# A delta-rule attention and rational feed-forward kernel: VectorE does a share of Pool's unit steps, in a fixed order, and ScalarE makes first halves

## The chip, the cores and the metric

The kernel runs on one core of a Trainium2 chip. The metric is the device time of one execution in microseconds; several executions of the same program are timed, and the median is given.

## The reference

Two computations follow one another. The first is attention by the delta rule over 4 batches, 8 heads, 768 tokens and 48 channels per head; a state matrix is carried from token to token:

```python
k_n = k / (np.linalg.norm(k, axis=-1, keepdims=True) + 1e-06)
for t in range(S):
    kt, vt, bt = (k_n[:, :, t], v[:, :, t], beta[:, :, t, None])
    y[:, :, t] = np.einsum('bhd,bhde->bhe', q[:, :, t], state)
    v_old = np.einsum('bhde,bhd->bhe', state, kt)
    state = state + bt[:, :, :, None] * np.einsum('bhd,bhe->bhde', kt, vt - v_old)
```

Its output, as 3072 tokens of 384 channels, is the input of a feed-forward layer with 2048 hidden channels, whose activation is a quotient of polynomials:

```python
h = x @ w_in
P = a[0] + a[1] * h + a[2] * h**2 + a[3] * h**3
Q = 1.0 + np.abs(b[0]) * np.abs(h) + np.abs(b[1]) * h**2
out = (P / (Q + 1e-06)) @ w_out
```

## The kernel before, in words

The 768 tokens are cut into 12 chunks of 64. A chunk of all four batches makes 256 token columns (TG). The hidden channels are cut into 8 slices of 256, so the feed-forward part has 96 **units**, each one chunk and one slice. Matrix products run on TensorE in float16; for accuracy each operand is held as two float16 halves, a first half (the value rounded) and a second half (what the rounding left), and a product takes three passes.

One unit n goes through four functions:

- `hidden(n)`: TensorE makes h in a PSUM tile `ph` (two such tiles). Line L806.
- `numerator(n)`: ACT takes z = |B1 h| (L824); DVE makes w = (z + B0) h (L826); ACT makes u = A3 h + a2 (L828) and then |w| (L829); DVE makes u = h u (L830) and u = (u + A1) h (L831). These three DVE steps read `ph`; L831 is the last to do so, and sets it free.
- `quotient(n)`: ACT makes r = 1 / (w + Q0) as an exponential of a negative logarithm (L842, L843). DVE makes the first half g of the quotient (L848), then g times the denominator (L849), then what is missing of the numerator (L853); all three have their two tile operands in SBUF. Pool turns that into the second half (L854).
- `accumulate(n)`: TensorE multiplies with w_out into `po` (L869); after a chunk's last slice ACT copies the sum out (L883).

For a share of the units, `by_pool` (slices 0, 4, 5 and 6 of chunks 2 to 10, 36 units), Pool takes a part of DVE's steps: it adds A0 to u (L835), so that DVE's L848 becomes the plain product L846, and it does the subtraction (L851) instead of L853.

Around it the attention part of later chunks runs interleaved, one eighth of a chunk per unit (`attention`): `keys_normalized` and `queries_transposed` put keys and queries, split into halves by `transposed`, into one SBUF tile `kn`, which a DMA on SyncE's queue (SP) writes to DRAM as `xdk` or `xdq` (L461); another DMA brings them back transposed. `key_products` multiplies the keys with themselves (tile `g`, L519) and splits the product into `gl`. In `transposed` and `key_products` the first half is made by Pool (L226, the parameter `hi` of `split16`), and the second half, a subtraction, by Pool too (L232). Other splits let ACT make the first half (L228, L230). Other names: `rr` is the residual, `z` a step of the triangular solve, `mm` the masked query products, `xT` the feed-forward input, `wai`, `wao` and `wsi` belong to the weights, which are prepared in the prologue, the first 150 us.

The engines each run their instructions in one fixed order. That order is not written out: a scheduler works it out when the program is built, from the order in the code, priorities (`tc.high_priority`) and its own estimate of when each instruction becomes ready.

Of the kernel before, what the change touches and what calls it, by code (L numbers as in the profile page):

```python
# [36 lines left out]
def kernel(  # L37
# [138 lines left out]
    def zeroed(n, shape, dtype, nm, part=lambda t: t, eng=nc.gpsimd):  # L176
        made = []
        for i in range(n):
# [41 lines left out]

    S16 = cpool.tile([P, HP, D], F32, name="S16")

    def split16(dst, src, scale=None, eng=None, hi=None):

        if hi is not None:
            hi.tensor_scalar(dst[0], src, 1.0 if scale is None else scale, 0.0, op0=ALU.mult, op1=ALU.add)  # L226
        elif scale is None:
            nc.scalar.copy(dst[0], src)  # L228
        else:
            nc.scalar.activation(dst[0], src, AF.Copy, scale=scale)  # L230
        if scale is None:
            (eng or nc.vector).tensor_sub(dst[1], src, dst[0])  # L232
# [280 lines left out]
    def key_products(c):  # L513
        d = info[c]
        gd = d["gd"] = dpool.tile([P, BS], F32, tag="gd", name=f"gd_{c}")
        pg = bank(ps_f, f"pg_{c}", C)
# [2 lines left out]
        nc.scalar.mul(by_pair(g), pg[2], -1.0)  # L519
# [296 lines left out]
    def numerator(n):  # L816

        c, f2 = divmod(n, NU)
        d = unit[n]
# [4 lines left out]
        nc.scalar.activation(z, ph, AF.Abs, scale=B1)  # L824
# [1 line left out]
        nc.vector.scalar_tensor_tensor(out=w, in0=z, scalar=B0, in1=ph, op0=ALU.add, op1=ALU.mult)  # L826
# [1 line left out]
        nc.scalar.activation(u, ph, AF.Identity, scale=A3, bias=a2)  # L828
        nc.scalar.activation(w, w, AF.Abs)  # L829
        nc.vector.tensor_mul(u, ph, u)  # L830
        nc.vector.scalar_tensor_tensor(out=u, in0=u, scalar=A1, in1=ph, op0=ALU.add, op1=ALU.mult)  # L831

        by_pool = 2 <= c < NCH - 1 and f2 in (0, 4, 5, 6)
        if by_pool:
            nc.gpsimd.tensor_scalar(u, u, A0, 1.0, op0=ALU.add, op1=ALU.mult)  # L835
        d.update(u=u, w=w, r=r, A0=A0, Q0=Q0, by_pool=by_pool)

    def quotient(n):

        d = unit[n]  # L840
        u, w, r, A0, Q0, by_pool = (d.pop(x) for x in ("u", "w", "r", "A0", "Q0", "by_pool"))
        nc.scalar.activation(r, w, AF.Ln, bias=Q0)  # L842
        nc.scalar.activation(r, r, AF.Exp, scale=-1.0)  # L843
        g = sb.tile([P, 2, 2, TG], F16, tag="mg", name=f"mg{n}", bufs=MB)
        if by_pool:
            nc.vector.tensor_mul(g[:, 0], u, r)  # L846
        else:
            nc.vector.scalar_tensor_tensor(out=g[:, 0], in0=u, scalar=A0, in1=r, op0=ALU.add, op1=ALU.mult)  # L848
        nc.vector.scalar_tensor_tensor(out=w, in0=w, scalar=Q0, in1=g[:, 0], op0=ALU.add, op1=ALU.mult)  # L849
        if by_pool:  # L850
            nc.gpsimd.tensor_sub(u, u, w)  # L851
        else:
            nc.vector.scalar_tensor_tensor(out=u, in0=u, scalar=A0, in1=w, op0=ALU.add, op1=ALU.subtract)  # L853
        nc.gpsimd.tensor_mul(g[:, 1], u, r)  # L854
# [192 lines left out]
```

## Time and profile before

| what | us |
|---|---|
| median of 3 runs | 851.33 |
| lowest and highest | 850.73 to 855.22 |
| the profiled execution | 851.73 |
| its span, first to last instruction | 849.4 |
| chunks 2 to 8 of the units, from 297.5 | 423.1 |
| chunks 9 and 10, from 720.6 | 83.5 |
| chunk 11, from 804.1 | 45.3 |

The stages start with the first L824 of their chunk. In rows by line, a group shows its line, engine, operation, out<-in by tile names, shape, count, then its busy time and the mean of one in ns, then the idle time of the engine before them with what ended it. In rows in order of time the first number is the start and the second the duration in us; a bracket holds the idle time before and its releaser. PE is TensorE's matmuls, PEld its weight loads, DVE VectorE, ACT ScalarE, POOL GpSimd, SP the queue that issues DMAs.

### The profile page before, as it was taken

Reading aid. Unit: us, or ns where it says so; the run is one execution under the profiler, and the core shown is the slowest. Engines: PE = TensorE matmul, PEld = TensorE weight load, DVE = VectorE, ACT = ScalarE, POOL = GpSimd, SP = SyncE. Lnnn points to the kernel's source line nnn. Section 1 sums busy time; section 2 is a strip of 40 time slices with the busy share of each in tenths; the row PEclk is TensorE's granted clock in tenths of the full one; section 3 lists DMA queues with packets and bytes.
Section 4 is the critical chain, followed back from the end, with each engine's and each line's share of the span. In section 5 each row is a group of like instructions: output and inputs, shape, how many; then the busy total and the mean of one; then the engine's idle time right before and its main releaser. Section 6 shows DMA issues by size and latency. Waiting matters only on the chain.

```text
span 849.4 us, 23212 instructions
## 1 busy us (share of the span) xinstructions
PE 625.6 (74%) x9264; PEld 491.3 (58%) x9264; DVE 761.0 (90%) x1369; ACT 589.5 (69%) x1242; POOL 466.9 (55%) x430
## 2 busy tenths in 40 slices
PE   0230425777788678888868869879879889999885
PEld 0220425656466467666756747657657767787563
DVE  5999898799799889889978898897999999999886
ACT  3766667748575675886774866767677867887774
POOL 7665665464436556565564655664756546454522
PEclk9855556988999899999999989989989999999999
DMA  8987989959899968959879498379587583300000
GB/s 230 259 198 148 221 157 172 149 117 148 155 172 147 175 123 160 151 102 193 144 140 176 85 183 149 66 158 165 89 159 129 97 139 58 72 2 20 1 20 19
DMA packets 466507, 111.46 MB, mean 131 GB/s; under 512 B 431328, under 2 KB 463072, under 8 KB 466400
## 3 DMA queue, kind: packets, MB, share of 16 engines
q1 hardware_dynamic: 464224, 108.83, 69.7%
q8 instruction: 72, 1.18, 0.6%
q10 hardware_dynamic: 2176, 1.17, 0.5%
q14 instruction: 35, 0.29, 0.1%
HBM read 40.47 MB, written 26.23 MB: 79 GB/s over the span
## 4 chain that ended last, share of the span: by engine, by line
DVE 41%; ACT 14%; DMA 12%; PE 11%; issue 8%; SPq 8%; POOL 3%; POOLq 0%; ACTq 0%; DVEq 0%
DVE mw L849 4%; PE ph L806 4%; PE po L869 4%; DVE w_out L327 3%; DVE mw L826 3%; DVE mg L848 3%; DVE mu L830 3%; DVE mu L831 3%; DVE mu L853 2%; ACT mu L828 2%; DVE mg L846 2%; SPq L609 2%; DVE z L234 2%; ACT mr L824 2%; ACT kp L764 2%
## 5 line engine op out<-in xcount | busy, mean ns | idle before, releaser
L806 PE MATMUL ph<-xT,w_in 128*128 128x256 f16 x1728 | 224.2, 283 | 37.1 <-DVE mu L831 33.8
L869 PE MATMUL po<-w_out,mg 128*128 128x384 f16 x1152 | 223.4, 339 | 33.5 <-POOL mg L854 27.3
L806 PEld LDWEIGHTS <-w_in 128*128 128x128 f16 x1728 | 172.0, 102 | 76.4 <-DVE mu L831 24.9
L854 POOL TENSOR_TENSOR mg<-mu,mr 128x512 f16<-128x512 f32 x96 | 135.3, 1410 | 106.5 <-DVE mu L853 50.9
L869 PEld LDWEIGHTS <-mg 128*128 128x128 f16 x1152 | 110.6, 101 | 105.5 <-POOL mg L854 34.1
L828 ACT ACTIVATE mu<-ph,coef,msc 128x512 f32<-128x512 f32 x96 | 74.7, 778 | 54.4 <-DVE mw L826 54.2
L849 DVE SCALAR_TENSOR_TENSOR mw<-mw,msc,mg 128x512 f32<-128x512 f32 x96 | 92.6, 965 | 0.5
L851 POOL TENSOR_TENSOR mu<-mu,mw 128x512 f32<-128x512 f32 x36 | 51.0, 1418 | 72.5 <-DVE mw L849 38.3
L824 ACT ACTIVATE mr<-ph,msc 128x512 f32<-128x512 f32 x96 | 64.9, 682 | 36.9 <-POOL mg L854 11.5
L403 PEld LDWEIGHTS <-kbd 128*128 128x128 f16 x1680 | 60.8, 104 | 35.2 <-issue 33.4
L826 DVE SCALAR_TENSOR_TENSOR mw<-mr,msc,ph 128x512 f32<-128x512 f32 x96 | 70.4, 737 | 10.7 <-ACT mr L824 10.6
L831 DVE SCALAR_TENSOR_TENSOR mu<-mu,msc,ph 128x512 f32<-128x512 f32 x96 | 70.8, 739 | 1.1
L830 DVE TENSOR_TENSOR mu<-ph,mu 128x512 f32<-128x512 f32 x96 | 65.2, 680 | 5.6 <-ACT mu L828 4.6
L842 ACT ACTIVATE mr<-mw,msc 128x512 f32<-128x512 f32 x96 | 69.4, 724 | 0.9
L403 PE MATMUL pu<-z,ebd 128*128 128x48 f16 x1728 | 52.7, 186 | 19.4 <-DVE z L234 15.4
L848 DVE SCALAR_TENSOR_TENSOR mg<-mu,msc,mr 128x512 f16<-128x512 f32 x60 | 58.9, 982 | 6.2 <-ACT mr L843 5.7
L403 PEld LDWEIGHTS <-ebd 128*128 128x128 f16 x1728 | 51.7, 98 | 22.0 <-issue 20.8
L843 ACT ACTIVATE mr<-mr 128x512 f32<-128x512 f32 x96 | 60.2, 630 | 0.7
L829 ACT ACTIVATE mw<-mw 128x512 f32<-128x512 f32 x96 | 60.0, 625 | 0.0
L853 DVE SCALAR_TENSOR_TENSOR mu<-mu,msc,mw 128x512 f32<-128x512 f32 x60 | 52.1, 869 | 0.2
L835 POOL TENSOR_SCALAR mu<-mu,msc 128x512 f32<-128x512 f32 x36 | 28.1, 782 | 40.5 <-DVE mu L831 28.3
L232 POOL TENSOR_TENSOR mm<-m,mm 128x1024 f16<-128x1024 f32 x12 | 31.1, 2589 | 32.7 <-ACT mm L228 30.5
(198 smaller groups left out, 1306.3 us busy)
## 6 DMA issues: line engine op xcount, KB each, us to landing
wsi<-in_moe_w_in_dram SPq DMA_DIRECT2D x24, 256.0 KB, 5.2
xdk<-kn SPq DMA_DIRECT2D x24, 256.0 KB, 3.7
kbd<-tk SPq DMA_DIRECT2D x24, 256.0 KB, 5.1
gd<-g SPq DMA_DIRECT2D x24, 256.0 KB, 3.5
wso<-in_moe_w_out_dram SPq DMA_DIRECT2D x32, 192.0 KB, 4.0
xdq<-kn SPq DMA_DIRECT2D x24, 256.0 KB, 3.6
mbd<-mm SPq DMA_DIRECT2D x24, 256.0 KB, 5.4
wc<-img SPq DMA_DIRECT2D x24, 256.0 KB, 4.8
```

Source lines behind the costliest of these rows:

```text
L403: nc.tensor.matmul(dst[p][:, h], head(bd, lp, p * H + h), head(rt, rp, p * H + h), start=start and n == 0 and h == 0, stop=stop and n == l ...
L806: nc.tensor.matmul(ph[:, i], w_in[:, f2, wp, cc, i * P : (i + 1) * P], x[:, xp, cc], start=k == 0, stop=k == 3 * NCC - 1,)
L824: nc.scalar.activation(z, ph, AF.Abs, scale=B1)
L826: nc.vector.scalar_tensor_tensor(out=w, in0=z, scalar=B0, in1=ph, op0=ALU.add, op1=ALU.mult)
L828: nc.scalar.activation(u, ph, AF.Identity, scale=A3, bias=a2)
L830: nc.vector.tensor_mul(u, ph, u)
L831: nc.vector.scalar_tensor_tensor(out=u, in0=u, scalar=A1, in1=ph, op0=ALU.add, op1=ALU.mult)
L842: nc.scalar.activation(r, w, AF.Ln, bias=Q0)
L848: nc.vector.scalar_tensor_tensor(out=g[:, 0], in0=u, scalar=A0, in1=r, op0=ALU.add, op1=ALU.mult)
L849: nc.vector.scalar_tensor_tensor(out=w, in0=w, scalar=Q0, in1=g[:, 0], op0=ALU.add, op1=ALU.mult)
L854: nc.gpsimd.tensor_mul(g[:, 1], u, r)
L869: nc.tensor.matmul(po[p], g[:, gp, i, p * P : (p + 1) * P], w_out[:, f2, wp, i], start=f2 == lo and i == 0 and k == 0, stop=f2 == hi - 1 a ...
```

## The change

It has three parts. Pool's L835 and L851 and the special product L846 go, so that VectorE does L848, L849 and L853 for all 96 units. VectorE's six steps of the units carry one order token, which makes them run in the order in which the code names them: the three of numerator(n), then the three of quotient(n-1), then those of numerator(n+1). And the first halves of keys, queries and key products are made by ACT instead of Pool (36 instructions); Pool keeps the subtractions.

```diff
-    def split16(dst, src, scale=None, eng=None, hi=None):
-        if hi is not None:
-            hi.tensor_scalar(dst[0], src, 1.0 if scale is None else scale, 0.0, op0=ALU.mult, op1=ALU.add)
-        elif scale is None:
+    def split16(dst, src, scale=None, eng=None):
+        if scale is None:
             nc.scalar.copy(dst[0], src)
...
             eng=nc.gpsimd,
-            hi=nc.gpsimd,
         )
...
-        split16([gl[..., i] for i in range(2)], g[:, :, : C - 16], eng=nc.gpsimd, hi=nc.gpsimd)
+        split16([gl[..., i] for i in range(2)], g[:, :, : C - 16], eng=nc.gpsimd)
...
+    def in_order(bi):
+        tc.stamp_issue_order_token(bi.ins, "unit")
...
-        nc.vector.scalar_tensor_tensor(out=w, in0=z, scalar=B0, in1=ph, op0=ALU.add, op1=ALU.mult)
+        in_order(nc.vector.scalar_tensor_tensor(out=w, in0=z, scalar=B0, in1=ph, op0=ALU.add, op1=ALU.mult))
...
-        by_pool = 2 <= c < NCH - 1 and f2 in (0, 4, 5, 6)
-        if by_pool:
-            nc.gpsimd.tensor_scalar(u, u, A0, 1.0, op0=ALU.add, op1=ALU.mult)
...
-        if by_pool:
-            nc.vector.tensor_mul(g[:, 0], u, r)
-        else:
-            nc.vector.scalar_tensor_tensor(out=g[:, 0], in0=u, scalar=A0, in1=r, op0=ALU.add, op1=ALU.mult)
...
-        if by_pool:
-            nc.gpsimd.tensor_sub(u, u, w)
-        else:
-            nc.vector.scalar_tensor_tensor(out=u, in0=u, scalar=A0, in1=w, op0=ALU.add, op1=ALU.subtract)
+        in_order(nc.vector.scalar_tensor_tensor(out=u, in0=u, scalar=A0, in1=w, op0=ALU.add, op1=ALU.subtract))
         nc.gpsimd.tensor_mul(g[:, 1], u, r)
```

The other VectorE steps of `numerator` and `quotient` are wrapped in `in_order` in the same way. The lines of the changed file differ by a few: L826, L830 and L831 are now L828, L832 and L833; L848, L849 and L853 are L843, L844 and L845; ACT's L824, L828, L829, L842 and L843 are L826, L830, L831, L840 and L841; L461 is L458.

How the order moves is seen at two places. The first is VectorE in chunk 11, at units 91 to 94; the number behind mw, mu, mg, mr and ph is the unit. Before:

```order
L848 SCALAR_TENSOR_TENSOR mg92_14005<-mu92_13951,msc_11_13624,mr92_13947 128x512
L849 SCALAR_TENSOR_TENSOR mw92_13949<-mw92_13949,msc_11_13624,mg92_14005 128x512
L830 TENSOR_TENSOR mu93_13998<-ph_93_13975,mu93_13998 128x512
L853 SCALAR_TENSOR_TENSOR mu92_13951<-mu92_13951,msc_11_13624,mw92_13949 128x512
L831 SCALAR_TENSOR_TENSOR mu93_13998<-mu93_13998,msc_11_13624,ph_93_13975 128x512
L826 SCALAR_TENSOR_TENSOR mw94_14043<-mr94_14041,msc_11_13624,ph_94_14022 128x512
L848 SCALAR_TENSOR_TENSOR mg93_14052<-mu93_13998,msc_11_13624,mr93_13994 128x512
```

The steps of two units alternate: between the first step of unit 94 (L826) and its second (L830, further on) stand L848 and L849 of unit 93. Now, on the same engine at the same place:

```order
L828 SCALAR_TENSOR_TENSOR mw92_13913<-mr92_13911,msc_11_13589,ph_92_13892 128x512
L832 TENSOR_TENSOR mu92_13915<-ph_92_13892,mu92_13915 128x512
L833 SCALAR_TENSOR_TENSOR mu92_13915<-mu92_13915,msc_11_13589,ph_92_13892 128x512
L843 SCALAR_TENSOR_TENSOR mg91_13922<-mu91_13868,msc_11_13589,mr91_13864 128x512
L844 SCALAR_TENSOR_TENSOR mw91_13866<-mw91_13866,msc_11_13589,mg91_13922 128x512
L845 SCALAR_TENSOR_TENSOR mu91_13868<-mu91_13868,msc_11_13589,mw91_13866 128x512
L828 SCALAR_TENSOR_TENSOR mw93_13960<-mr93_13958,msc_11_13589,ph_93_13939 128x512
```

The first and the second step of unit 92 stand directly behind one another, then its third, and only then the three of the quotient of unit 91.

The second place is where keys of chunk 7 follow queries of chunk 6 into `kn` (kn0 in the rows). Before, on Pool:

```order
L226 TENSOR_SCALAR kn0_109<-q_6_5318 128x2x8x48
L851 TENSOR_TENSOR mu24_5619<-mu24_5619,mw24_5617 128x512
L232 TENSOR_TENSOR kn0_109<-q_6_5318,kn0_109 128x2x8x48
L854 TENSOR_TENSOR mg24_5754<-mu24_5619,mr24_5615 128x512
L854 TENSOR_TENSOR mg25_6007<-mu25_5747,mr25_5743 128x512
L232 TENSOR_TENSOR rr_5_6277<-v_5_4061,rr_5_6277 128x768
L226 TENSOR_SCALAR kn0_109<-k_7_5424 128x2x8x48
```

The cast of the keys, which must wait until the queries' DMA has read `kn`, stood in Pool's queue, with only Pool's work behind it. Now, on ACT:

```order
L226 CAST kn0_109<-q_6_5315 128x2x8x48
L841 ACTIVATE mr24_5611<-mr24_5611 128x512
L627 ACTIVATE sc_6_5687<-sc_6_5687 128x1
L830 ACTIVATE mu25_5742<-ph_25_5719,coef_99,msc_3_5313 128x512
L831 ACTIVATE mw25_5740<-mw25_5740 128x512
L826 ACTIVATE mr26_5991<-ph_26_5972,msc_3_5313 128x512
L840 ACTIVATE mr25_5738<-mw25_5740,msc_3_5313 128x512
L841 ACTIVATE mr25_5738<-mr25_5738 128x512
L875 ACTIVATE ob_2_5967<-po_2_0_0_5059,kp_2_0_4180 128x384
L875 ACTIVATE ob_2_5967<-po_2_0_1_5060,kp_2_0_4180 128x384
L226 CAST kn0_109<-k_7_5420 128x2x8x48
L830 ACTIVATE mu26_5995<-ph_26_5972,coef_99,msc_3_5313 128x512
```

The same cast is now in ACT's queue, nine instructions behind the cast of the queries, and ACT's steps of unit 26 stand behind it.

More of the change, by code (lines that the diff above doesn't have):

```diff
@@ L829, in numerator @@
         nc.scalar.activation(w, w, AF.Abs)
-        nc.vector.tensor_mul(u, ph, u)
-        nc.vector.scalar_tensor_tensor(out=u, in0=u, scalar=A1, in1=ph, op0=ALU.add, op1=ALU.mult)
-        by_pool = 2 <= c < NCH - 1 and f2 in (0, 4, 5, 6)
-        if by_pool:
-            nc.gpsimd.tensor_scalar(u, u, A0, 1.0, op0=ALU.add, op1=ALU.mult)
-        d.update(u=u, w=w, r=r, A0=A0, Q0=Q0, by_pool=by_pool)
+        in_order(nc.vector.tensor_mul(u, ph, u))
+        in_order(nc.vector.scalar_tensor_tensor(out=u, in0=u, scalar=A1, in1=ph, op0=ALU.add, op1=ALU.mult))
+        d.update(u=u, w=w, r=r, A0=A0, Q0=Q0)
     def quotient(n):
         d = unit[n]
-        u, w, r, A0, Q0, by_pool = (d.pop(x) for x in ("u", "w", "r", "A0", "Q0", "by_pool"))
+        u, w, r, A0, Q0 = (d.pop(x) for x in ("u", "w", "r", "A0", "Q0"))
         nc.scalar.activation(r, w, AF.Ln, bias=Q0)
@@ L844, in quotient @@
         g = sb.tile([P, 2, 2, TG], F16, tag="mg", name=f"mg{n}", bufs=MB)
-        if by_pool:
-            nc.vector.tensor_mul(g[:, 0], u, r)
-        else:
-            nc.vector.scalar_tensor_tensor(out=g[:, 0], in0=u, scalar=A0, in1=r, op0=ALU.add, op1=ALU.mult)
-        nc.vector.scalar_tensor_tensor(out=w, in0=w, scalar=Q0, in1=g[:, 0], op0=ALU.add, op1=ALU.mult)
-        if by_pool:
-            nc.gpsimd.tensor_sub(u, u, w)
-        else:
-            nc.vector.scalar_tensor_tensor(out=u, in0=u, scalar=A0, in1=w, op0=ALU.add, op1=ALU.subtract)
+        in_order(nc.vector.scalar_tensor_tensor(out=g[:, 0], in0=u, scalar=A0, in1=r, op0=ALU.add, op1=ALU.mult))
+        in_order(nc.vector.scalar_tensor_tensor(out=w, in0=w, scalar=Q0, in1=g[:, 0], op0=ALU.add, op1=ALU.mult))
+        in_order(nc.vector.scalar_tensor_tensor(out=u, in0=u, scalar=A0, in1=w, op0=ALU.add, op1=ALU.subtract))
         nc.gpsimd.tensor_mul(g[:, 1], u, r)
```

## The prediction

> **What bounds the kernel now.** I read the busy times of the page first, then the busy time by stage, then the groups of instructions by line, then the instructions in order of time in the last stage, and last the waits.
>
> ```profile
> PE 625.6 (74%) x9264; PEld 491.3 (58%) x9264; DVE 761.0 (90%) x1369; ACT 589.5 (69%) x1242; POOL 466.9 (55%) x430
> ```
>
> VectorE (DVE) is busy for 761.0 of 849.4 us; no other engine is above 74%. By stage (columns: window, its length, then busy time of PE, PEld, DVE, ACT, POOL with counts, TensorE's clock, DMA share, GB/s):
>
> ```profile
> 297.50:720.60 423.10, 357.38 (x5630) 282.76 (x5626) 385.76 (x631) 301.30 (x605) 249.74 (x203) 0.94 0.75 134
> 720.60:804.10 83.50, 78.84 (x984) 61.15 (x983) 76.08 (x117) 67.91 (x134) 40.66 (x34) 1.00 0.12 25
> ```
>
> The first row holds token chunks 2 to 8, the second 9 and 10; chunk 11 follows. VectorE is busy for 91% of both. What fills it are six steps per unit, 96 units:
>
> ```profile
> L849 DVE SCALAR_TENSOR_TENSOR mw<-mw,msc,mg 128x512 f32<-128x512 f32 x96 | 92.6, 965 | 0.5
> L826 DVE SCALAR_TENSOR_TENSOR mw<-mr,msc,ph 128x512 f32<-128x512 f32 x96 | 70.4, 737 | 10.7 <-ACT mr L824 10.6
> L830 DVE TENSOR_TENSOR mu<-ph,mu 128x512 f32<-128x512 f32 x96 | 65.2, 680 | 5.6 <-ACT mu L828 4.6 <-POOL mm L232 0.7
> L848 DVE SCALAR_TENSOR_TENSOR mg<-mu,msc,mr 128x512 f16<-128x512 f32 x60 | 58.9, 982 | 6.2 <-ACT mr L843 5.7
> L853 DVE SCALAR_TENSOR_TENSOR mu<-mu,msc,mw 128x512 f32<-128x512 f32 x60 | 52.1, 869 | 0.2
> L846 DVE TENSOR_TENSOR mg<-mu,mr 128x512 f16<-128x512 f32 x36 | 32.7, 908 | 5.1 <-ACT mr L843 4.3 <-POOL mu L835 0.7
> ```
>
> The steps that read ph (PSUM) take 737 and 680 ns. Those with two SBUF inputs have the same size but mean 869 to 982. One case shows where the rest goes; first VectorE, then Pool:
>
> ```profile
> 512.30 2.14 DVE L849 SCALAR_TENSOR_TENSOR mw<-mw,msc,mg 128x512 f32<-128x512 f32 x1
> ```
>
> ```profile
> 512.06 1.84 POOL L232 TENSOR_TENSOR rr<-v,rr 128x768 f16<-128x768 f32 x1
> ```
>
> The step began inside a Pool instruction, which ended at 513.90, and itself ended at 514.44, about 0.55 us after it: it stood still while Pool worked. The undisturbed sizes and the spacing of the steps are in the last stage:
>
> ```profile
> 830.92 0.74 DVE L826 SCALAR_TENSOR_TENSOR mw<-mr,msc,ph 128x512 f32<-128x512 f32 x1
> 831.58 0.75 DVE L848 SCALAR_TENSOR_TENSOR mg<-mu,msc,mr 128x512 f16<-128x512 f32 x1
> 831.70 0.78 ACT L828 ACTIVATE mu<-ph,coef,msc 128x512 f32<-128x512 f32 x1 [0.88 <-DVE mw L826]
> 832.37 0.75 DVE L849 SCALAR_TENSOR_TENSOR mw<-mw,msc,mg 128x512 f32<-128x512 f32 x1
> 833.04 0.68 DVE L830 TENSOR_TENSOR mu<-ph,mu 128x512 f32<-128x512 f32 x1
> 833.64 0.74 DVE L853 SCALAR_TENSOR_TENSOR mu<-mu,msc,mw 128x512 f32<-128x512 f32 x1
> 834.30 0.74 DVE L831 SCALAR_TENSOR_TENSOR mu<-mu,msc,ph 128x512 f32<-128x512 f32 x1
> 834.96 0.74 DVE L826 SCALAR_TENSOR_TENSOR mw<-mr,msc,ph 128x512 f32<-128x512 f32 x1
> ```
>
> This is one whole unit period, 4.04 us (834.96 - 830.92), with no idle time on VectorE. An independent next step starts 0.66 us after the one before it (833.64 to 834.30), a step that needs the result just made 0.79 us after (831.58 to 832.37). ScalarE (ACT) starts L828 only 0.04 us after L826 has ended, and VectorE's L830 needs L828's result. Here the steps of the unit ahead, L848 and L849, stand in that hole.
>
> **The change part by part.** *Work moved to VectorE.* 36 L853 more, at 0.66 us of spacing: 23.8 us. 36 L846 become L848 forms, 0.74 for 0.68 us: 2.2 us. Together **+26 us**, on the engine that sets the end. The same steps leave Pool:
>
> ```profile
> L854 POOL TENSOR_TENSOR mg<-mu,mr 128x512 f16<-128x512 f32 x96 | 135.3, 1410 | 106.5 <-DVE mu L853 50.9 <-ACT mr L842 11.8 <-PE po L869 7.1
> L851 POOL TENSOR_TENSOR mu<-mu,mw 128x512 f32<-128x512 f32 x36 | 51.0, 1418 | 72.5 <-DVE mw L849 38.3 <-ACT mu L828 18.1 <-DVE sf L744 6.2
> L835 POOL TENSOR_SCALAR mu<-mu,msc 128x512 f32<-128x512 f32 x36 | 28.1, 782 | 40.5 <-DVE mu L831 28.3 <-DVE xs L742 4.8 <-DVE pr L552 4.8
> L226 POOL TENSOR_SCALAR gl<-g 128x768 f16<-128x768 f32 x12 | 13.4, 1119 | 8.4 <-ACT g L519 8.0
> L226 POOL TENSOR_SCALAR kn<-k 128x768 f16<-128x768 f32 x12 | 11.3, 944 | 21.1 <-DMA xdq<-kn 21.0
> L226 POOL TENSOR_SCALAR kn<-q 128x768 f16<-128x768 f32 x12 | 10.9, 912 | 0.7
> ```
>
> *Stalls that go.* With 0.75, 0.75, 0.74 and 0.68 us as undisturbed times, the four SBUF steps lose to Pool 96 x 0.215 + 60 x 0.232 + 60 x 0.129 + 36 x 0.228 = 20.6 + 13.9 + 7.7 + 8.2 = 50.4 us. What is taken from Pool (L851, L835 and the 36 casts of L226) is 114.7 of its 466.9 us, a quarter: **-12 us**, with 0 and twice that, -25, as bounds, since a stall needs a meeting of the two. Nearly all of Pool's rest in the units is L854. In chunk 11 only L854 runs on Pool:
>
> ```profile
> L849 DVE SCALAR_TENSOR_TENSOR mw<-mw,msc,mg 128x512 f32<-128x512 f32 x8 | 7.1, 883 | 0.2
> L848 DVE SCALAR_TENSOR_TENSOR mg<-mu,msc,mr 128x512 f16<-128x512 f32 x8 | 6.4, 802 | 1.7 <-ACT mr L843 1.5
> ```
>
> There it costs 8 x 0.133 + 8 x 0.052 = 1.5 us, so 18 us over twelve chunks. In the new order L854 becomes ready when the last step of a unit (now L845) ends, and the next three unit steps all read ph, so a 1.27 us L854 meets nothing that it stops, unless Pool is late with attention work. I take two thirds: **-12 us** (bounds 0 and -18).
>
> *Steps that wait for one another.* The fixed order puts ph's two products, then the quotient's three steps, each behind the step that it needs: three pairs at 0.73 to 0.79 us where the old order of chunk 11 has one. Counted in the new order, 127 such pairs stand without a row between, against 52 before; 75 x 0.12 us is 9. I take **+8 us** (0 to +9).
>
> *The hole behind the first step.* From L826's start to L830's start at least 0.74 + 0.04 + 0.78 = 1.56 us pass, 0.90 more than the usual spacing. The other unit's steps fill it now; in the new order only attention steps may. I went through all 96 holes in both orders, gave each row inside the mean of its group without stalls, and summed what was missing to 0.9 us: 36 us in the new order, 3.5 in the old. Half of the new sum, 17.7 us, falls on the last 24 units, where attention work has run out. **+33 us**, lower bound the last 24 units alone (+17).
>
> *The casts on ACT.* 36 casts at about the size of this one, in the row of rr:
>
> ```profile
> L828 ACT ACTIVATE mu<-ph,coef,msc 128x512 f32<-128x512 f32 x96 | 74.7, 778 | 54.4 <-DVE mw L826 54.2
> L842 ACT ACTIVATE mr<-mw,msc 128x512 f32<-128x512 f32 x96 | 69.4, 724 | 0.9
> L824 ACT ACTIVATE mr<-ph,msc 128x512 f32<-128x512 f32 x96 | 64.9, 682 | 36.9 <-POOL mg L854 11.5 <-PE ph L806 11.4 <-DVE msc L790 10.0
> L843 ACT ACTIVATE mr<-mr 128x512 f32<-128x512 f32 x96 | 60.2, 630 | 0.7
> L829 ACT ACTIVATE mw<-mw 128x512 f32<-128x512 f32 x96 | 60.0, 625 | 0.0
> L883 ACT ACTIVATE ob<-po,kp 128x384 f32<-128x384 f32 x24 | 12.9, 582 | 5.7 <-PE po L869 5.7
> L228 ACT CAST rr<-v 128x768 f16<-128x768 f32 x12 | 9.9, 828 | 10.0 <-DVE v L679 10.0
> ```
>
> That is 36 x 0.83 = 30 us on an engine with 260 us free: nothing, as long as it has room. But a cast of keys overwrites kn, which the queries' DMA (xdq) still reads. Before, that wait stood on Pool, in these pairs from the cast of queries to the cast of keys:
>
> ```profile
> 429.97 0.83 POOL L226 TENSOR_SCALAR kn<-q 128x768 f16<-128x768 f32 x1
> ...
> 442.45 0.83 POOL L226 TENSOR_SCALAR kn<-k 128x768 f16<-128x768 f32 x1 [3.35 <-DMA xdq<-kn]
> ```
>
> ```profile
> 491.93 0.82 POOL L226 TENSOR_SCALAR kn<-q 128x768 f16<-128x768 f32 x1
> ...
> 500.82 0.83 POOL L226 TENSOR_SCALAR kn<-k 128x768 f16<-128x768 f32 x1 [3.92 <-DMA xdq<-kn]
> ```
>
> From the end of one cast to the start of the next 8.1 to 11.7 us pass (Pool's subtraction, SP's queue, the landing). In ACT's new queue, at the place shown above, two halves of units stand between (L828, L829, L824, L842, twice L843, twice L883: 5.2 us). So ACT would stand 3 to 6.5 us at up to nine places in the loop, less the idle third that it has anyway; queued behind the cast are the next unit's L828 and L829, for which VectorE's second step waits. VectorE has the three quotient steps, 2 us, to go on with. I take 0.8 us a place, **+7 us** (0 to +58).
>
> *What absorbs.* VectorE is idle for 37.3 us in chunks 2 to 8 (423.1 - 385.8). Part of that is time in which ACT or a DMA is behind, and shrinks when VectorE has more to do. I take half, **-20 us** with rounding up for the other stages (bounds 0 and -37). In the prologue the casts change engines in place, 0.83 for 0.94 us, which I count as nothing. Pool's lighter queue shortens its tail too, L851's 1.4 us before L854, but the last units had none of that.
>
> Sum: 26 - 12 - 12 + 8 + 33 + 7 - 20 = +30 us. The profiled execution took 851.73 us, 2.3 more than its span of 849.4; the median of the runs is 851.33, 0.4 lower. 851.33 + 30 = **881 us**.
>
> **The rivals.** *Faster: Pool's stalls were the price.* If the fixed order and the emptier Pool take away all 50 us of unit stalls, with 15 more in the attention steps (which meet the same Pool instructions), and attention fills every hole but those of the last 24 units, the sum is 26 - 65 + 8 + 18 = -13: 838 us. For it speaks that each stall ends with a Pool instruction; against it that attention's own Pool work (keys, queries, rr, mm: unchanged) makes much of them, and that chunk 11, with 1.5 us to win, has 8 x 0.90 to lose. The Trainium skill (SBUF — State Buffer, section SBUF: two separate sides) calls the pair of ports that VectorE and Pool share an exclusive lock, held for a whole instruction, which a VectorE instruction with two SBUF inputs needs; the 2.14 us row agrees, and by that rule alone the change should win. Chance 0.12.
>
> *No difference.* VectorE's idle time, 88 us in all, takes in the moved work and the holes outside the tail: 26 - 24 + 8 + 33 + 7 less 50 is 0, 851 us. Against it: the stage of chunks 9 and 10 has 83.5 - 76.1 = 7.4 us of idle time for 16 holes of up to 0.90. Chance 0.08.
>
> *Slower still: keys on ACT.* If each of the nine waits costs 3.3 us instead of 0.8, it is 30 instead of 7: 904 us. It decides from the point where the queries' DMA lands later than ACT and VectorE have queued work, about 7 us after the cast. Chance 0.15.
>
> That the order is not what the change says is excluded: all 576 steps stand in it.
>
> **How the numbers follow.** My forecast has 0.65. A measurement can tell about 0.5%, 4.3 us, from no change. Slower by more: 0.65 + 0.15 = 0.80; the same 0.08; faster 0.12. The range reaches from 850, which takes in no difference, to 908, which takes in the third rival; faster and costlier waits are left out, some 2 in 10. The forecast's own range, with the absorption at its -37 or at 0, is 864 to 901.
>
> **What would show it.** In the profile after: VectorE busy about 765 us or more, its four SBUF groups closer to 0.75 (the L844 group, formerly L849, near 0.87); idle time ahead of L832 (formerly L830), put down to ACT mu, about 35 us instead of 4.6; a unit period of about 5 us in chunk 11 instead of 4.04; ACT waiting at kn L226 for xdq. I am wrong if L832's idle time stays under 10 us, or if the last stage is not longer by 5 us or more.

## The result and the profile after

The kernel with the change takes 889.05 us (median of 4 runs, 885.33 to 891.33), the kernel before 853.28 us (median of 4 runs, 850.73 to 855.31). The ratio is 1.0441, 95% interval 1.0407 to 1.0475: the change costs 35.8 us. The profiled execution took 891.33 us with a span of 889.6, which is 40.2 more than the span before. The working below goes by the two spans.

The page's first part, after:

```profile
PE 636.9 (72%) x9264; PEld 494.4 (56%) x9264; DVE 758.8 (85%) x1405; ACT 612.8 (69%) x1278; POOL 341.7 (38%) x322
```

VectorE has 36 instructions more and is busy 2.2 us less (761.0 before). So the whole loss is idle time of VectorE: 130.8 us (889.6 - 758.8) against 88.4. Its unit steps after, from the groups by line (last column: idle time just before them):

```profile
L844 DVE SCALAR_TENSOR_TENSOR mw<-mw,msc,mg 128x512 f32<-128x512 f32 x96 | 81.3, 846 | 1.1
L845 DVE SCALAR_TENSOR_TENSOR mu<-mu,msc,mw 128x512 f32<-128x512 f32 x96 | 77.2, 804 | 1.4
L843 DVE SCALAR_TENSOR_TENSOR mg<-mu,msc,mr 128x512 f16<-128x512 f32 x96 | 76.9, 801 | 0.0
...
L832 DVE TENSOR_TENSOR mu<-ph,mu 128x512 f32<-128x512 f32 x96 | 65.9, 686 | 49.9 <-ACT mu L830 49.7
...
L492 DVE TENSOR_REDUCE nrm<-sq 128x16 f32<-128x768 f32 x12 | 11.4, 949 | 9.5 <-ACT sq L491 9.4
```

The three SBUF steps fell from means of 965, 869 and 982 ns to 846, 804 and 801: their stalls went from 50.4 us to 20.2, which is 96 x (0.096 + 0.064 + 0.051) but for rounding. But ahead of L832, the second step of a unit, VectorE stands idle for 49.9 us, nearly all of it until ACT's L830 (5.6 before, ahead of L830 as it was called then). The last row, the norm of the keys, is taken up further down. One whole period in chunk 11, in order of time on three engines (a bracket holds the idle time before):

```profile
856.87 0.74 DVE L828 SCALAR_TENSOR_TENSOR mw<-mr,msc,ph 128x512 f32<-128x512 f32 x1
857.12 1.27 POOL L846 TENSOR_TENSOR mg<-mu,mr 128x512 f16<-128x512 f32 x1 [4.02 <-DVE mu L845]
857.64 0.78 ACT L830 ACTIVATE mu<-ph,coef,msc 128x512 f32<-128x512 f32 x1 [2.14 <-DVE mw L828]
858.52 0.69 DVE L832 TENSOR_TENSOR mu<-ph,mu 128x512 f32<-128x512 f32 x1 [0.92 <-ACT mu L830]
859.25 0.75 DVE L833 SCALAR_TENSOR_TENSOR mu<-mu,msc,ph 128x512 f32<-128x512 f32 x1
859.91 0.75 DVE L843 SCALAR_TENSOR_TENSOR mg<-mu,msc,mr 128x512 f16<-128x512 f32 x1
860.69 0.75 DVE L844 SCALAR_TENSOR_TENSOR mw<-mw,msc,mg 128x512 f32<-128x512 f32 x1
861.48 0.75 DVE L845 SCALAR_TENSOR_TENSOR mu<-mu,msc,mw 128x512 f32<-128x512 f32 x1
862.15 0.74 DVE L828 SCALAR_TENSOR_TENSOR mw<-mr,msc,ph 128x512 f32<-128x512 f32 x1
```

The period is 5.28 us against 4.04. ACT's L830 begins only when VectorE's L828 has ended, and VectorE has nothing it may do until L830 is done: 0.92 us of hole. The other 0.3 us are dependent pairs, 0.73 to 0.79 us apart. Pool's product runs in the hole and stops nobody: the SBUF steps here take 0.75 us. By stage (chunks 2 to 8, then 9 and 10, then 11; the columns are those of the prediction):

```profile
295.80:740.70 444.90, 361.17 (x5598) 284.29 (x5597) 390.63 (x659) 314.55 (x625) 163.62 (x127) 0.95 0.75 128
740.70:832.40 91.70, 79.87 (x933) 58.44 (x931) 78.20 (x126) 67.96 (x135) 21.97 (x17) 1.00 0.12 22
832.40:889.60 57.20, 39.72 (x249) 23.51 (x247) 40.46 (x56) 28.26 (x47) 13.02 (x10) 0.92 0.06 14
```

The stages grew by 21.8, 8.2 and 11.9 us. In chunks 9 to 11, where attention work has run out, the holes sum to 16.8 us (4.3, 5.2 and 7.3). Before that most holes are short and a few are long. If each hole is counted up to 0.95 us, just over the 0.92 of the rows above, they make 36.8 us; the other 13.1 us lie beyond 0.95, in eight long ones. The longest, VectorE and ACT in order of time:

```profile
704.15 0.74 DVE L828 SCALAR_TENSOR_TENSOR mw<-mr,msc,ph 128x512 f32<-128x512 f32 x1
706.65 1.36 ACT L226 CAST mm<-m 128x1024 f16<-128x1024 f32 x1 [4.81 <-DMA mbd<-mm]
707.85 0.78 ACT L830 ACTIVATE mu<-ph,coef,msc 128x512 f32<-128x512 f32 x1
708.73 0.69 DVE L832 TENSOR_TENSOR mu<-ph,mu 128x512 f32<-128x512 f32 x1 [3.84 <-ACT mu L830]
```

ACT's queue stood at a cast of mm for a DMA, L830 was queued behind it, and VectorE waited with it. Seven holes are longer than 1.3 us. In five of them ACT still waited for a DMA after the unit's L828 had begun: three times at sq (the load of queries), once at y, once at mm. In the other two it was late with work queued ahead of L830 (in the one that ends at 588.02 with y, xT and sq, in the one that ends at 644.30 with ob and L841). The waits that bear on this:

```profile
DVE mu L832 <- ACT mu L830: 49.7, 47, 3.8
ACT kn L226 <- DMA xdq<-kn: 18.2, 8, 4.3
ACT sq L491 <- DMA k<-in_k_dram: 16.1, 6, 4.8
ACT y L718 <- DMA out_dram<-ob: 11.7, 6, 6.6
```

The wait of the keys' cast (kn, L226) is there as foretold, 18.2 us at eight places, but it is the last wait ahead of L830 in none of the seven long holes. In the hole that ends at 280.64 it stands earlier in ACT's queue, and ACT waited again behind it, for the load of queries.

### The profile page after: what moved, and what is told of

It reads as the page before. It is cut to its first block, busy times and chain, and to the rows that moved or that the text cites. A ratio compares the mean times of both kernels' runs of the same rounds, so it can differ in the third digit from the quotient of the medians.

```text
span 889.6 us, 23165 instructions
## 1 busy us (share of the span) xinstructions
PE 636.9 (72%) x9264; PEld 494.4 (56%) x9264; DVE 758.8 (85%) x1405; ACT 612.8 (69%) x1278; POOL 341.7 (38%) x322
## 4 chain that ended last, share of the span: by engine, by line
DVE 36%; DMA 19%; PE 15%; SPq 11%; ACT 11%; issue 6%; POOL 2%; DVEq 0%; ACTq 0%; POOLq 0%
PE po L861 5%; PE ph L808 4%; DVE mu L845 4%; DVE mw L844 4%; DVE mu L833 3%; DVE mu L832 3%; DVE w_out L325 3%; DVE mg L843 3%; DMA tk<-xdk 3%; DVE mw L828 3%; ACT mu L830 3%; DMA tq<-xdq 2%; SPq L119 2%; DMA mbd<-mm 2%; DMA q<-in_q_dram 2%
## 5 line engine op out<-in xcount | busy, mean ns | idle before, releaser
L861 PE MATMUL po<-w_out,mg 128*128 128x384 f16 x1152 | 228.2, 337 | 34.3 <-POOL mg L846 29.6
L846 POOL TENSOR_TENSOR mg<-mu,mr 128x512 f16<-128x512 f32 x96 | 124.0, 1291 | 323.3 <-DVE mu L845 298.2
L861 PEld LDWEIGHTS <-mg 128*128 128x128 f16 x1152 | 108.6, 101 | 107.9 <-POOL mg L846 42.6
L830 ACT ACTIVATE mu<-ph,coef,msc 128x512 f32<-128x512 f32 x96 | 74.3, 774 | 89.7 <-DVE mw L828 89.7
L832 DVE TENSOR_TENSOR mu<-ph,mu 128x512 f32<-128x512 f32 x96 | 65.9, 686 | 49.9 <-ACT mu L830 49.7
L844 DVE SCALAR_TENSOR_TENSOR mw<-mw,msc,mg 128x512 f32<-128x512 f32 x96 | 81.3, 846 | 1.1
L845 DVE SCALAR_TENSOR_TENSOR mu<-mu,msc,mw 128x512 f32<-128x512 f32 x96 | 77.2, 804 | 1.4
L843 DVE SCALAR_TENSOR_TENSOR mg<-mu,msc,mr 128x512 f16<-128x512 f32 x96 | 76.9, 801 | 0.0
L833 DVE SCALAR_TENSOR_TENSOR mu<-mu,msc,ph 128x512 f32<-128x512 f32 x96 | 71.4, 743 | 2.0
L826 ACT ACTIVATE mr<-ph,msc 128x512 f32<-128x512 f32 x96 | 64.8, 678 | 10.4 <-DVE msc L787 4.4
L828 DVE SCALAR_TENSOR_TENSOR mw<-mr,msc,ph 128x512 f32<-128x512 f32 x96 | 71.0, 740 | 0.8 <-ACT mr L826 0.8
L840 ACT ACTIVATE mr<-mw,msc 128x512 f32<-128x512 f32 x96 | 68.9, 717 | 0.1
L841 ACT ACTIVATE mr<-mr 128x512 f32<-128x512 f32 x96 | 60.2, 627 | 0.9
L831 ACT ACTIVATE mw<-mw 128x512 f32<-128x512 f32 x96 | 59.5, 620 | 0.0
L401 PEld LDWEIGHTS <-wbd 128*128 128x128 f16 x1152 | 37.4, 101 | 34.1 <-issue 28.9
L232 DVE SCALAR_TENSOR_TENSOR z<-pu,zmask,z 128x768 f16<-128x768 f32 x36 | 36.3, 1008 | 0.6 <-ACT z L228 0.4
```

Source lines behind the costliest of these rows:

```text
L401: nc.tensor.matmul(dst[p][:, h], head(bd, lp, p * H + h), head(rt, rp, p * H + h), start=start and n == 0 and h == 0, stop=stop and n == l ...
L828: in_order(nc.vector.scalar_tensor_tensor(out=w, in0=z, scalar=B0, in1=ph, op0=ALU.add, op1=ALU.mult))
L832: in_order(nc.vector.tensor_mul(u, ph, u))
L833: in_order(nc.vector.scalar_tensor_tensor(out=u, in0=u, scalar=A1, in1=ph, op0=ALU.add, op1=ALU.mult))
L843: in_order(nc.vector.scalar_tensor_tensor(out=g[:, 0], in0=u, scalar=A0, in1=r, op0=ALU.add, op1=ALU.mult))
L844: in_order(nc.vector.scalar_tensor_tensor(out=w, in0=w, scalar=Q0, in1=g[:, 0], op0=ALU.add, op1=ALU.mult))
```

## The experiments

**Theories.** The main one (the hole): the fixed order puts a unit's first two steps side by side, and the time in which ACT makes u between them stays empty; the other two parts cost little. Rivals: the casts on ACT hold up ACT's queue; the work taken from Pool costs what it weighs. Then, for a remedy: if the hole is the cause, a fixed order without it should be fast.

### Each part alone, and in pairs

Six kernels complete the eight combinations of the three parts with the kernel before and the one after. O is the fixed order, T is VectorE taking back Pool's share, A is the casts on ACT. **O alone** (b_order):

```diff
+    def in_order(bi):
+        tc.stamp_issue_order_token(bi.ins, "unit")
...
-        nc.vector.tensor_mul(u, ph, u)
+        in_order(nc.vector.tensor_mul(u, ph, u))
```

All VectorE steps of a unit are wrapped like this; Pool keeps its share and the casts.

> The kernel before with the fixed order of VectorE's unit steps alone; Pool keeps its share and its first halves. If the hole behind the first step is the cause: 30 to 40 us of idle time ahead of the product with ph, put down to ACT mu, and 875 to 890 us. If the moved work or the casts on ACT are the cause: 845 to 860 us, and under 10 us of that idle time.

Measured: 887.40 us, ratio 1.0411 (1.0362 to 1.0460). The order alone costs as much as the whole change. The second step, and one long hole, from the groups and the order of time of b_order:

```profile
L835 DVE TENSOR_TENSOR mu<-ph,mu 128x512 f32<-128x512 f32 x96 | 65.8, 686 | 52.8 <-ACT mu L833 52.6
```

```profile
520.42 0.74 DVE L831 SCALAR_TENSOR_TENSOR mw<-mr,msc,ph 128x512 f32<-128x512 f32 x1
525.10 0.90 ACT L721 ACTIVATE y<-py,sc 128x768 f32<-128x768 f32 x1 [5.94 <-DMA out_dram<-ob]
525.90 0.77 ACT L833 ACTIVATE mu<-ph,coef,msc 128x512 f32<-128x512 f32 x1
526.77 0.69 DVE L835 TENSOR_TENSOR mu<-ph,mu 128x512 f32<-128x512 f32 x1 [5.62 <-ACT mu L833]
```

The hole is as large, 52.8 us (30 to 40 were expected), with long ones as well (15.9 us beyond 0.95), although no cast of keys is on ACT here. The long holes are therefore not the casts' doing.

**T alone** (b_take):

```diff
-        by_pool = 2 <= c < NCH - 1 and f2 in (0, 4, 5, 6)
+        by_pool = False
```

> The kernel before with all unit steps of Pool's share back on VectorE, no fixed order, first halves still on Pool. If the moved work is the cause: 26 us more work and little less stall, 865 to 880 us. If the hole is: the added work is paid by stalls that go and by idle time, 846 to 862 us, with under 10 us of idle time ahead of the product with ph.

Measured: 862.15 us, 1.0115 (1.0076 to 1.0154). VectorE is busy 779.8 us, 18.8 more than before, and the span is 860.0, 10.6 more. The time lies between the two ranges that were expected, next to the one for the hole. The second step waits little:

```profile
L830 DVE TENSOR_TENSOR mu<-ph,mu 128x512 f32<-128x512 f32 x96 | 65.3, 681 | 8.7 <-ACT mu L828 8.5
```

**A alone** (b_act):

```diff
-            hi=nc.gpsimd,
...
-        split16([gl[..., i] for i in range(2)], g[:, :, : C - 16], eng=nc.gpsimd, hi=nc.gpsimd)
+        split16([gl[..., i] for i in range(2)], g[:, :, : C - 16], eng=nc.gpsimd)
```

> The kernel before with the first halves of keys, queries and key products on ACT alone. If the casts are the cause: ACT waits about 18 us for the queries' DMA as in the changed kernel, and the time is 865 to 885 us. If the hole is: the waits are taken up by steps of other units that the scheduler puts into them, 847 to 860 us.

Measured: 852.44 us, 1.0020 (0.9993 to 1.0047), no difference, with nearly the same wait on ACT as in the kernel after:

```profile
ACT kn L228 <- DMA xdq<-kn: 17.0, 6, 4.5
```

**T and A** (b_take_act: the kernel after without the order), **O and T** (b_order_take: the kernel after with the casts on Pool), **O and A** (b_order_act: the kernel after with Pool's share kept):

```diff
-        in_order(nc.vector.tensor_mul(u, ph, u))
+        nc.vector.tensor_mul(u, ph, u)
```

> The changed kernel without its fixed order: VectorE has all steps, ACT the first halves. If the hole is the cause: 848 to 864 us. If the moved work and the casts are: 878 to 892 us, as the changed kernel.

```diff
             eng=nc.gpsimd,
+            hi=nc.gpsimd,
```

The first half of the key products goes back to Pool in the same way.

> The changed kernel with the first halves back on Pool: fixed order, VectorE has all steps. If the casts on ACT cost what their waits are long (18 us, and five long holes of 2.6 to 3.8 us): 868 to 878 us, and no hole longer than 1.5 us. If only the short holes count: 882 to 892 us.

```diff
+        by_pool = 2 <= c < NCH - 1 and f2 in (0, 4, 5, 6)
```

> The kernel before with the fixed order and the first halves on ACT; Pool keeps its share of the unit steps. If the hole and the casts are the cause and the moved work is paid by stalls: 880 to 895 us. If the moved work matters: 855 to 872 us.

Measured: 865.62 us for T and A, 891.43 for O and T, 878.53 for O and A. The first is 1.6 us over the range expected if the hole is the cause; the last lies between its two ranges, 1.5 us under the one for the hole and the casts. The measured ratios with their intervals, and how each profiled span is made up on VectorE. The stalls are part of the busy time: the excess of the SBUF steps over 0.75, 0.75, 0.74 and 0.68 us, as the prediction counted them. The hole is the idle time ahead of the second step; the rest is span less busy time less hole.

| kernel | ratio (95%) | span | busy | its stalls | hole | other idle |
|---|---|---|---|---|---|---|
| before | 1 | 849.4 | 761.0 | 50.4 | 5.6 | 82.8 |
| T | 1.0115 (1.0076-1.0154) | 860.0 | 779.8 | 48.8 | 8.7 | 71.5 |
| A | 1.0020 (0.9993-1.0047) | 855.2 | 754.5 | 43.6 | 13.0 | 87.7 |
| T A | 1.0162 (1.0108-1.0217) | 869.0 | 774.4 | 51.3 | 11.4 | 83.2 |
| O | 1.0411 (1.0362-1.0460) | 881.6 | 765.2 | 40.5 | 52.8 | 63.6 |
| O T | 1.0465 (1.0416-1.0513) | 894.1 | 778.9 | 37.5 | 50.7 | 64.5 |
| O A | 1.0302 (1.0252-1.0353) | 877.4 | 741.7 | 25.7 | 46.7 | 89.0 |
| O T A (after) | 1.0441 (1.0407-1.0475) | 889.6 | 758.8 | 20.2 | 49.9 | 80.9 |

The four kernels without O have a hole of 5.6 to 13.0 us, the four with it 46.7 to 52.8. By the quotients of the ratios O costs 4.1% alone and 2.7 to 3.5% on top of the other parts, T 1.2 and 1.4% without the order and 0.5 and 1.3% with it; A lies between +0.5% and -1.0%. For O with T no hole over 1.5 us had been expected if the casts make the long ones; there are two of 5.3 us, so the long holes don't need the casts on ACT.

Two rows of b_order_take, for later: ACT's wait for the load of the keys, and the group of the keys' norm.

```profile
ACT sq L494 <- DMA k<-in_k_dram: 6.3, 3, 2.9
```

```profile
L495 DVE TENSOR_REDUCE nrm<-sq 128x16 f32<-128x768 f32 x12 | 11.4, 946 | 1.5 <-ACT sq L494 1.5
```

The table also shows two exchanges. With the order, 18 to 19 us of other idle time are taken in (82.8 to 63.6 and 64.5). With the casts on ACT in addition, VectorE's busy time falls by 23.5 and 20.1 us, and its other idle time grows by 25.4 and 16.4.

### The hole taken out in two ways

**ACT's step first** (a_swap): in the kernel after, ACT's u is written ahead of VectorE's first step. Nothing else differs.

```diff
+        u = sb.tile([P, 2, TG], F32, tag="mu", name=f"mu{n}", bufs=MB)
+        nc.scalar.activation(u, ph, AF.Identity, scale=A3, bias=a2)
         w = sb.tile([P, 2, TG], F32, tag="mw", name=f"mw{n}", bufs=MB)
         in_order(nc.vector.scalar_tensor_tensor(out=w, in0=z, scalar=B0, in1=ph, op0=ALU.add, op1=ALU.mult))
-        u = sb.tile([P, 2, TG], F32, tag="mu", name=f"mu{n}", bufs=MB)
-        nc.scalar.activation(u, ph, AF.Identity, scale=A3, bias=a2)
```

> The changed kernel with one line moved: ACT makes its product of ph right behind its first one, ahead of VectorE's first step in the code, so that VectorE's second step no longer waits for ACT behind its first. If the hole is the cause: idle time ahead of the second step falls from 50 to under 12 us and the time to 840 to 860 us. If the order as such, the moved work or the casts are: 880 us or more.

Measured: 859.78 us, 1.0075 (1.0049 to 1.0101), against 1.0441 for the same kernel without the swap. Its first and second steps, from the groups by line:

```profile
L845 DVE SCALAR_TENSOR_TENSOR mu<-mu,msc,mw 128x512 f32<-128x512 f32 x96 | 89.4, 932 | 1.4
...
L830 DVE SCALAR_TENSOR_TENSOR mw<-mr,msc,ph 128x512 f32<-128x512 f32 x96 | 71.0, 740 | 11.2 <-ACT mu L828 11.1
...
L832 DVE TENSOR_TENSOR mu<-ph,mu 128x512 f32<-128x512 f32 x96 | 65.4, 681 | 0.0
```

The second step never waits. The wait is now ahead of the first step and is 11.2 us in all, since ACT can make u while VectorE still does the quotient of the unit before. The period in chunk 11 is 4.28 us, 0.24 over 4.04: the dependent pairs. The SBUF steps lose more to Pool again (45.2 us of stalls in all against 20.2; L845's mean is 932 against 804 ns), which gives back part of the gain.

**A fixed order that alternates** (a_inter): one token still, but the quotient steps of unit n-1 are written between those of unit n. For this ACT's two steps of the reciprocal (logarithm and exponential) are written at the end of numerator(n), one unit earlier in the code than in the kernel after, so ACT's code is not quite in the same order as there. The lines below show VectorE's part and Pool's.

```diff
         in_order(nc.vector.scalar_tensor_tensor(out=w, in0=z, scalar=B0, in1=ph, op0=ALU.add, op1=ALU.mult))
...
+        p = unit.get(n - 1)
+        if p:
+            in_order(nc.vector.scalar_tensor_tensor(out=p["g"][:, 0], in0=p["u"], scalar=p["A0"], in1=p["r"], op0=ALU.add, op1=ALU.mult))
+            in_order(nc.vector.scalar_tensor_tensor(out=p["w"], in0=p["w"], scalar=p["Q0"], in1=p["g"][:, 0], op0=ALU.add, op1=ALU.mult))
         in_order(nc.vector.tensor_mul(u, ph, u))
+        if p:
+            in_order(nc.vector.scalar_tensor_tensor(out=p["u"], in0=p["u"], scalar=p["A0"], in1=p["w"], op0=ALU.add, op1=ALU.subtract))
+            nc.gpsimd.tensor_mul(p["g"][:, 1], p["u"], p["r"])
         in_order(nc.vector.scalar_tensor_tensor(out=u, in0=u, scalar=A1, in1=ph, op0=ALU.add, op1=ALU.mult))
```

> The changed kernel with another fixed order: first step of unit n, then two steps of the quotient of unit n-1, then the second step of unit n, the last of the quotient, the third of unit n. ACT's code is in the same order as the changed kernel's. If the hole is the cause: it is filled, 845 to 862 us. If a fixed order as such costs the time: 875 us or more.

Measured: 839.84 us, 0.9861 (0.9813 to 0.9910): 1.4% faster than the kernel before, and better than expected. One period in chunk 11, VectorE alone, and the second step's group and ACT's wait:

```profile
809.61 0.74 DVE L828 SCALAR_TENSOR_TENSOR mw<-mr,msc,ph 128x512 f32<-128x512 f32 x1
810.27 0.76 DVE L834 SCALAR_TENSOR_TENSOR mg<-mu,msc,mr 128x512 f16<-128x512 f32 x1
811.07 0.75 DVE L835 SCALAR_TENSOR_TENSOR mw<-mw,msc,mg 128x512 f32<-128x512 f32 x1
811.74 0.68 DVE L836 TENSOR_TENSOR mu<-ph,mu 128x512 f32<-128x512 f32 x1
812.34 0.74 DVE L838 SCALAR_TENSOR_TENSOR mu<-mu,msc,mw 128x512 f32<-128x512 f32 x1
813.00 0.74 DVE L840 SCALAR_TENSOR_TENSOR mu<-mu,msc,ph 128x512 f32<-128x512 f32 x1
813.65 0.74 DVE L828 SCALAR_TENSOR_TENSOR mw<-mr,msc,ph 128x512 f32<-128x512 f32 x1
```

```profile
L836 DVE TENSOR_TENSOR mu<-ph,mu 128x512 f32<-128x512 f32 x96 | 65.4, 681 | 7.5 <-ACT mu L830 7.4
```

```profile
ACT kn L226 <- DMA xdq<-kn: 19.4, 9, 4.7
```

The period is 4.04 us again (813.65 - 809.61), the hole 7.5 us. ACT's wait for the queries' DMA is as long as ever, 19.4 us, beside a faster kernel.

### How much of the hole must be filled, and the other parts in that order

**One step in the hole** (i_one): as a_inter, but only the first quotient step stands behind a unit's first step; the other two follow its third (the diff is against the kernel after; ACT's code is that of a_inter).

```diff
+        if p:
+            in_order(nc.vector.scalar_tensor_tensor(out=p["g"][:, 0], in0=p["u"], scalar=p["A0"], in1=p["r"], op0=ALU.add, op1=ALU.mult))
         in_order(nc.vector.tensor_mul(u, ph, u))
         in_order(nc.vector.scalar_tensor_tensor(out=u, in0=u, scalar=A1, in1=ph, op0=ALU.add, op1=ALU.mult))
+        if p:
+            in_order(nc.vector.scalar_tensor_tensor(out=p["w"], in0=p["w"], scalar=p["Q0"], in1=p["g"][:, 0], op0=ALU.add, op1=ALU.mult))
+            in_order(nc.vector.scalar_tensor_tensor(out=p["u"], in0=p["u"], scalar=p["A0"], in1=p["w"], op0=ALU.add, op1=ALU.subtract))
+            nc.gpsimd.tensor_mul(p["g"][:, 1], p["u"], p["r"])
```

> The alternating fixed order with only one quotient step in the hole instead of two: 0.66 of the 0.90 us are filled. If the hole sets the time in proportion: 8 to 20 us of idle time ahead of the second step, and 848 to 868 us, between the alternating order (840) and the changed kernel (889). If the time comes from something else that the alternation changes: 838 to 844 us or 880 and more.

Measured: 861.48 us, 1.0099 (1.0063 to 1.0135). Time and hole (10.8 us) are both in the ranges expected, but the hole is not the reason: it is 3.3 us larger than in a_inter, while the kernel is 2.4% slower. From the groups of i_one, and a period in chunk 11 with Pool:

```profile
L834 DVE SCALAR_TENSOR_TENSOR mg<-mu,msc,mr 128x512 f16<-128x512 f32 x95 | 111.8, 1177 | 1.3 <-ACT mr L842 1.2
...
L835 DVE TENSOR_TENSOR mu<-ph,mu 128x512 f32<-128x512 f32 x96 | 65.2, 679 | 10.8 <-ACT mu L830 10.7
```

```profile
834.67 0.74 DVE L828 SCALAR_TENSOR_TENSOR mw<-mr,msc,ph 128x512 f32<-128x512 f32 x1
834.92 1.26 POOL L840 TENSOR_TENSOR mg<-mu,mr 128x512 f16<-128x512 f32 x1 [3.55 <-DVE mu L839]
835.33 1.41 DVE L834 SCALAR_TENSOR_TENSOR mg<-mu,msc,mr 128x512 f16<-128x512 f32 x1
836.66 0.68 DVE L835 TENSOR_TENSOR mu<-ph,mu 128x512 f32<-128x512 f32 x1
...
839.48 0.74 DVE L828 SCALAR_TENSOR_TENSOR mw<-mr,msc,ph 128x512 f32<-128x512 f32 x1
```

The quotient's last step now ends a unit, Pool's product starts 0.25 us into the next unit's first step, and the SBUF step behind that meets it: it starts at 835.33 inside Pool's instruction, which ends at 836.18, and itself ends at 836.74, 1.41 us instead of 0.75. The next period begins at 839.48, 4.81 us after this one. A stall that filled the hole has taken the hole's place: 65.1 us of stalls, VectorE busy for 789.8. This is what the Trainium skill says of the pair of ports that VectorE and Pool share (SBUF — State Buffer, section SBUF: two separate sides): of a VectorE instruction with two SBUF inputs and a Pool instruction that reads SBUF, the one that starts first holds the pair for the whole instruction and the other waits. The rows agree in the main: the step ends 0.56 us after Pool's, so most of its 0.75 us lies behind it. In a_inter two steps that read ph stand between the quotient's last and the next SBUF step, and L834 takes 0.76 us there.

**The casts back on Pool** (i_pool), **the share back on Pool** (i_share_act), **both** (i_share), all with a_inter's order:

```diff
+            hi=nc.gpsimd,
```

> The alternating fixed order with the first halves of keys, queries and key products back on Pool. If the casts on ACT cost time through their wait for the queries' DMA: 825 to 835 us. If they cost nothing or help by freeing Pool: 838 to 850 us.

```diff
+                nc.gpsimd.tensor_sub(p["u"], p["u"], p["w"])
...
+            nc.gpsimd.tensor_scalar(u, u, A0, 1.0, op0=ALU.add, op1=ALU.mult)
```

> The alternating fixed order, the first halves on ACT, but Pool keeps its share of the unit steps. If the two parts add up: about as much faster than the alternating order with all steps on VectorE (840) as the moved work costs, 826 to 836 us. If Pool's lighter queue is what the alternating order lives on: 840 to 855 us.

```diff
+            hi=nc.gpsimd,
...
+                nc.gpsimd.tensor_sub(p["u"], p["u"], p["w"])
...
+            nc.gpsimd.tensor_scalar(u, u, A0, 1.0, op0=ALU.add, op1=ALU.mult)
```

> The kernel before in all but the alternating fixed order: Pool keeps its share of the unit steps and the first halves. If the moved work costs about 11 us when no hole stands in the way, as it did without a fixed order (862 for 851): 825 to 840 us. If VectorE's work is paid by stalls that go: 840 to 852 us.

The stalls in this table and of i_one are those of 95 units, since the last unit's quotient has lines of its own.

| alternating order with | us | ratio (95%) | span | busy | its stalls | hole | other idle |
|---|---|---|---|---|---|---|---|
| T A (a_inter) | 839.84 | 0.9861 (0.9813-0.9910) | 836.5 | 751.0 | 30.2 | 7.5 | 78.0 |
| T (i_pool) | 844.08 | 0.9879 (0.9847-0.9911) | 839.7 | 769.9 | 39.0 | 5.3 | 64.5 |
| A (i_share_act) | 838.41 | 0.9821 (0.9780-0.9861) | 835.6 | 732.7 | 27.3 | 5.3 | 97.6 |
| neither (i_share) | 842.30 | 0.9870 (0.9833-0.9908) | 840.9 | 751.3 | 42.4 | 1.6 | 88.0 |

All four beat the kernel before, by 1.2 to 1.8%. i_pool and i_share came out as expected if the part costs nothing or is paid by stalls that go; i_share_act lies between its two ranges. The four intervals overlap, so with this order neither T nor A has a clear price. i_share_act, with Pool's share kept and the casts on ACT, has the lowest time. The exchange of the first table is here too: the casts on ACT take 18.9 and 18.6 us off VectorE's busy time and add 13.5 and 9.6 of idle time.

## Why the prediction was right, step by step

It said +30 us and the change cost 35.8 (the span 40.2). The mechanism that it named first, the hole behind the first step, is shown: the order alone makes it, a swap of two instructions in the code takes most of the cost away, and an order that fills it takes all of it. By the spans, the prediction had +2 us for VectorE's busy time (26 less 24), +33 for the hole and -5 for the rest (8 + 7 - 20). Measured are -2.2, +44.3 and -1.9. So it was the hole that made the sum too small; that the other two came so near is partly luck, since their parts did not come as foretold.

- **The hole, +33.** Measured 49.9 - 5.6 = +44.3. What was worked out from 0.9 us a hole was right: 36.8 us for 36, and 16.8 for 17.7 on the last 24 units. Missed were the 13.1 us of longer holes. Before, a late L830 found VectorE busy with other steps, and no hole was longer than 0.97 us; in the fixed order DMA waits in ACT's queue (sq, y, mm) reach VectorE.
- **Work moved, +26, and absorption, -20.** The prediction's +26 with none of the stalls gone would be 787.0; T alone gives 779.8, +18.8. The groups of the unit steps sum to 27.6 us more in T (470.3 against 442.7), so the moved work itself was sized about right, and 8.8 us less are VectorE's other steps and overlaps of neighbours. The hole grew by 3.1, other idle time took in 11.3 (82.8 to 71.5), and the span grew by 10.6. Absorption alone was nearly as sized: 18.3 us from before to O T. In the kernel after it does not show, 82.8 to 80.9, because the casts gave 16.4 back.
- **Stalls that go, -12 and -12.** In all 30.2 us went. The step that failed is the first: it put the gain on Pool's work taken away by its length, of which T is 79.1 us (L851 and L835) and the casts 35.6. T saves 1.6 us of stalls alone, 3.0 on top of O and 5.5 on top of O A, and on top of A it adds 7.7. The order saves 9.9 alone and 31.1 on top of T A. The casts save 6.8 alone, 14.8 on top of O and 17.3 on top of O T, and on top of T they add 2.5. The gain hangs on the parts together, not on the length of the work taken away.
- **The casts on ACT, +7.** The wait came (18.2 us at eight places, 3 to 6.5 foretold for each, 2.3 measured), but it didn't act where it was put, ahead of the second step: it ends no long hole, and the casts on top of O T change the time by -0.2%, inside the noise. On top of O T the casts save 20.1 us of busy time and add 16.4 of idle time elsewhere. Half of that, 8.0 us, is the wait of the keys' norm for ACT's square of the keys (9.5 us after, 1.5 in O T), where ACT itself waits for the load of the keys, 16.1 us against 6.3. The wait of the norm grows by about as much in the other pairs with and without the casts on ACT (8.4 against 2.4 alone, 9.2 against 2.5 on top of T, 9.6 against 1.5 on top of O), but not with the alternating order and T (2.8 against 3.3). Whether the casts make those loads late was not tried.
- **Dependent pairs, +8.** Chunk 11 shows them: 5.28 - 4.04 = 1.24 us, of which 0.92 is the hole and 0.32 the pairs. a_swap has 0.24 without the hole. Times 96, that would be 23 to 31 us, but other steps stand between the pairs until chunk 9; their sum over the kernel wasn't measured.

The rivals: that Pool's stalls were the price, with the change faster, needed the holes filled. Of the 50.4 us of stalls 30.2 did go, and in a_inter, where the holes are filled as well, the same parts give 0.9861 with 20.2 us of stalls fewer than before. The rival was right that stalls go, though not all 50, and wrong about this order. Keys on ACT as the cause of a slower kernel falls: O alone is as slow without them, and A alone changes nothing (1.0020). No difference needed 50 us of absorption; at most 19 came.

Of the signs named for the profile, the L844 group (0.87 said, 0.846 measured), the period (about 5, 5.28) and the wait at kn held; VectorE's busy time (765 or more) came out at 758.8 and the idle time ahead of L832 (about 35) at 49.9, for the reasons above.

What stays open: why ACT's L830 waits for VectorE's L828 at all, when both only read ph. In all 96 units it starts at least 0.03 us after L828's end, and in a_swap, where the code names it first, VectorE's step starts at least 0.03 us after ACT's end instead. No run here shows what makes them take turns. And since every edit makes the scheduler lay the attention work anew, differences of a few us between two of these kernels can't be given to the one part that differs.

## What to carry to other kernels

A fixed order on the busiest engine should be read for what stands between a step and the next one that needs another engine's answer to it: here the time of ACT's step, up to 0.9 us in a unit and 49.9 us in all with the long waits, cost more than the 31.1 us of stalls that the order saved with the other two parts in place. An order that puts independent steps there keeps most of both gains (a hole of 7.5 us, stalls of 30.2, and 0.9861 against 1.0441 for the same work). And before a fixed order is kept, follow which steps meet another engine's instruction on a shared port: i_one and a_inter differ by the place of two steps and by 2.4%.

## What the runs showed of the hardware that was not expected

- How much VectorE's SBUF steps lose to Pool hangs on the order more than on Pool's load. With Pool's work the same, the stalls are 30.2 us in a_inter, 20.2 in the kernel after and 65.1 in i_one (Pool busy for 345.6, 341.7 and 343.2 us).
- The 36 casts on Pool, 35.6 us of work in the kernel before, cost VectorE 18.6 to 23.5 us of busy time in the four pairs with a fixed order, and 5.4 to 6.5 in the two without, beside the same kernel with the casts on ACT. With a fixed order half or more of it comes back as idle time of VectorE elsewhere, 9.6 to 25.4 us.
